# Decoding weights in place, squaring into another tile, a shorter layer norm, and a new table of event times

## The chip, the cores and the metric

The kernel runs on one core of a Trainium2 chip. The metric is the device time of one execution in microseconds (us), the median of several runs. Five engines work side by side: TensorE (PE, with its weight loads shown apart as PEld), VectorE (DVE), ScalarE (ACT), GpSimd (POOL) and SyncE (SP, whose queue issues all DMAs here). Each works through its own list of instructions in order and waits on semaphores for the others.

## The reference

A linear attention with decay over 4 batches, 8 heads, 768 steps and 48 channels gives 3072 tokens of 384 channels. Two feed-forward layers follow.

```python
def _attn_ref(r, k, v, w, u):
    ...
        cur = np.einsum('bhd,bhe->bhde', u[None] * kt, vt)
        y[:, :, t] = np.einsum('bhd,bhde->bhe', rt, state + cur)
        state = wt[:, :, :, None] * state + np.einsum('bhd,bhe->bhde', kt, vt)

def _moe_ref(x, w_in, w_out, g_ln):          # 384 -> 1024 -> 384
    h = x @ w_in
    e = np.exp(h - np.max(h, axis=-1, keepdims=True))
    solu = h * e / (np.sum(e, axis=-1, keepdims=True) + 1e-09)
    mu = np.mean(solu, axis=-1, keepdims=True)
    var = np.mean((solu - mu) ** 2, axis=-1, keepdims=True)
    return ((solu - mu) / np.sqrt(var + 1e-06) * g_ln) @ w_out

def _moe2_ref(x, w_in, w_out):               # 384 -> 2048 -> 384
    r = np.maximum(x @ w_in, 0.0)
    return (r * r) @ w_out
```

The weights arrive as 64-bit floats. The kernel reads each as two 32-bit words (`low`, `high`) and rebuilds a 32-bit float from their bits.

## The kernel before

Tokens go through in 24 tiles of 128 (`st`) and 12 groups of two tiles (`g`). Every float32 product is made of three matmuls on a high and a low part (`mm3`).

Per tile, attention runs as `prep_k` (two scans on DVE over the decays, behind the load of `wt`), `prep_r`, `prep_chk`, `prep_c*`, `u1` (transposes `pk`), `u3` (`pat`), `u2` (products `pm`, then the state's update on DVE), `u4` (outputs `py`, summed to `tk` or `early`) and `u5` (transposes `px`, split on ACT and DVE into `xh` and `xl`). The first layer is `m1_in` (18 matmuls `ph`, the logits, in PSUM banks of tag `h`), then maximum, exponential, product `z`, Square, variance, power -1/2 on POOL, `m1_ln` (normalises `z`) and `ln_T` (8 transposes `pl`, split into `lnh` and `lnl`). Per group, `m1_out` makes three products `po` of 24 matmuls, split into `x2h` and `x2l`; `m2_in(g, j)` makes 18 matmuls `p` and from them `gh` and `gl`; `m2_out(g, j)` adds 12 matmuls into `acc` (for group 0 `acch`, which takes the same banks of tag `h` as the logits); j runs from 0 to 7.

All weights stay in SBUF. They are loaded raw and decoded during the first tiles: `split_w1i`, `split_w1o` and `split_w2` call `decode` for pieces of 512 columns (384 for `w1o`), 38 pieces in all. A piece takes two or three ACT passes, two or three DVE passes and one POOL subtraction. It is rebuilt in a tile `t` of the tag `raw`, which has `RAWB` = 4 buffers and also holds `gh`, `gl` and the output tiles:

```python
        t = p2.tile([128, 512], F32, tag="raw", name="t", bufs=RAWB)[:, 0:n]
        nc.scalar.activation(out=t, in_=high.bitcast(F32), func=AF.Copy, scale=2.0 ** -112)
```

The order is written as a list of events: `at(t, f, *args)` enters a function with a time, the list is sorted by time, and the functions are called in that order. The tile framework's scheduler may still interleave the instructions of neighbouring events. Tables (`SPLIT_AT`, `ATT_AT`, `FIRST_AT`, `ATT_OFF`) set the times; `SHIFT` is read by `at` and empty.

Of the kernel before, what the change touches and what calls it, by code (L numbers as in the profile page):

```python
# [52 lines left out]
def body(ctx: ExitStack, tc: tile.TileContext, wrk, tok, vst, u, w1i, w1o, gln, w2, gen, vt, ug, out):  # L53
    nc = tc.nc
# [82 lines left out]
    def split_w1i(k):
        raw = raw_t.pop(("i", k))  # L140
        for a in range(0, FF1, 512):
            b = a + 512
            decode(raw[:, a:b], w1i_s[:, 0, k, a:b], w1i_s[:, 1, k, a:b])

    def split_w1o(k):
        raw = raw_t.pop(("o", k))
        for i in range(4):
            q = 4 * k + i
            decode(raw[:, i * DM:(i + 1) * DM], w1o_s[:, 0, q], w1o_s[:, 1, q], gcol[:, q:q + 1])

    def split_w2(j):
        if j < 7:
            raw = raw_t.pop(("2", j))
            parts = [raw[:, i:i + 512] for i in range(0, 1536, 512)]
        else:
            src = w2[j].rearrange("p (n t) -> p n t", t=2)
            parts = []
            for tag, a, n in (("lnh", 0, 1024), ("lnl", 1024, 512)):
# [2 lines left out]
                parts += [raw[:, i:i + 512] for i in range(0, n, 512)]
        w2_t[j] = wp.tile([128, 2, 1536], F32R, tag=f"w2_{j}", name="w2_s")
        for i, part in enumerate(parts):
            s = slice(i * 512, (i + 1) * 512)
            decode(part, w2_t[j][:, 0, s], w2_t[j][:, 1, s])

# [186 lines left out]
    def m1_in(st):  # L353
        xh, xl = x_t.pop(st)
        ph = ps_h.tile([128, FF1], F32, tag="h", name="ph")
        for n in range(2):
# [17 lines left out]
        z_t[st] = (z, nmz, rs, va, qq)  # L374

    def m1_ln(st):
        z, nmz, rs, va, qq = z_t[st]
        nc.vector.tensor_tensor(out=qq, in0=va, in1=rs, op=ALU.mult)
        nc.vector.tensor_scalar(out=z, in0=z, scalar1=nmz, scalar2=qq, op0=ALU.add, op1=ALU.mult)

    def ln_T(st):
# [2 lines left out]
        if g not in ln_t:
            ln_t[g] = (
                p1.tile([128, 8, 256], F32R, tag="lnh", name="lnh"),
                p1.tile([128, 8, 256], F32R, tag="lnl", name="lnl"),
            )
# [129 lines left out]
    wk = [(split_w1i, k) for k in range(3)] + [(split_w1o, k) for k in range(2)]
    wk += [(split_w2, j) for j in range(8)]
    refill = {0: 0, 1: 1, 2: 2, 6: 3, 5: 4, 8: 5, 7: 6}  # L520
    for n, (f, k) in enumerate(wk):
        at(SPLIT_AT[n], f, k)
# [147 lines left out]
```

## Time and profile before

| | us |
|---|---|
| three timed runs | 836.26, 837.32, 840.6 |
| median | 837.32 |
| the profiled execution, its own time | 832.33 |
| its span in the profile | 830.6 |

The profiled execution was 5.0 us below the median of the timed runs. 1.7 us of its time lie outside the span. In the profile an instruction is named by line, engine, operation and `out<-in`; a time in brackets is how long its engine stood idle just before it, and what ended that.

### The profile page before, as it was taken

What the parts mean: (1) busy time and instruction counts of PE and PEld (TensorE: products, weight loads), DVE (VectorE), ACT (ScalarE), POOL (GpSimd) and SP (SyncE); (2) the same over time, 40 slices, a digit from 0 to 9 for tenths busy, and PEclk for the clock granted to TensorE, in tenths of its full rate; (3) what the DMA queues carried; (4) which work ended last, traced back from release to release, by engine and by line L of the source; (5) the groups of instructions that cost most, each with busy time, mean ns of one, the idle gap of its engine ahead of it and who ended that gap; (6) DMA issues with size and microseconds to landing.
All of it is one profiled execution on the core that took longest, in us unless ns stands there. A gap on an engine that the chain in (4) does not pass through costs nothing.

```text
span 830.6 us, 17797 instructions
## 1 busy us (share of the span) xinstructions
PE 754.0 (91%) x7610; PEld 702.6 (85%) x7610; DVE 520.8 (63%) x974; ACT 338.2 (41%) x631; POOL 152.3 (18%) x146
## 2 busy tenths in 40 slices
PE   3566859899999999999999999999999999999996
PEld 3355759799788998988998999988998998999996
DVE  6899996775746556556556557556557557544332
ACT  4576566444423433333433333333333342333232
POOL 3635453231011011011011011011011011010000
PEclk9967978999999999999999999999999999999999
DMA  9940552221122202112112112112112112010000
GB/s 329 357 141 20 186 191 77 54 63 54 49 82 63 55 29 82 54 29 83 54 30 82 54 30 82 54 30 83 54 39 73 54 49 63 2 39 2 1 20 24
DMA packets 20568, 60.51 MB, mean 73 GB/s; under 512 B 3585, under 2 KB 12929, under 8 KB 18817
## 3 DMA queue, kind: packets, MB, share of 16 engines
q1 hardware_dynamic: 20480, 59.29, 22.5%
q8 instruction: 62, 1.02, 0.5%
q14 instruction: 26, 0.20, 0.1%
HBM read 54.56 MB, written 4.72 MB: 71 GB/s over the span
## 4 chain that ended last, share of the span: by engine, by line
PE 53%; DVE 22%; DMA 9%; ACT 6%; issue 3%; POOL 3%; SPq 2%; DVEq 0%; ACTq 0%; POOLq 0%
PE p L85 16%; PE acc L85 13%; DMA wt<-in_wrk 9%; PE po L85 7%; PE ph L85 7%; DVE q L232 3%; PE py L85 3%; PE pl L394 2%; DVE q L240 2%; SPq L207 2%; DVE p L433 2%; DVE t L114 2%; DVE t L112 1%; DVE stat L362 1%; PE acch L85 1%
## 5 line engine op out<-in xcount | busy, mean ns | idle before, releaser
L85 PE MATMUL p<-x2h,w_s 128*128 128x256 f32 x1152 | 222.8, 284 | 0.0
L85 PEld LDWEIGHTS p<-x2h,w_s 128*128 128x128 f32 x1152 | 184.3, 190 | 2.2
L85 PE MATMUL acc<-w_s,gh 128*128 128x384 f32 x704 | 185.3, 343 | 0.9 <-ACT gh L432 0.8
L85 PE MATMUL p<-x2l,w_s 128*128 128x256 f32 x576 | 162.2, 282 | 0.0
L85 PEld LDWEIGHTS acc<-w_s,gh 128*128 128x128 f32 x704 | 122.8, 189 | 2.9 <-ACT gh L432 1.3
L85 PE MATMUL acc<-w_s,gl 128*128 128x384 f32 x352 | 118.9, 339 | 1.0 <-DVE gl L434 1.0
L85 PE MATMUL po<-lnh,w1o_s 128*128 128x256 f32 x576 | 107.8, 282 | 7.9 <-DVE x2l L414 6.6
L85 PEld LDWEIGHTS p<-x2l,w_s 128*128 128x128 f32 x576 | 109.2, 190 | 1.0 <-DVE x2l L414 0.2
L431 ACT ACTIVATE r<-p 128x512 f32<-128x512 f32 x96 | 57.0, 594 | 126.0 <-PE p L85 95.5
L433 DVE TENSOR_TENSOR p<-p,r 128x512 f32<-128x512 f32 x96 | 66.7, 695 | 62.1 <-ACT r L431 62.0
L85 PE MATMUL ph<-w1i_s,xh 128*128 128x512 f32 x288 | 96.2, 415 | 6.5 <-ACT w1i_s L118 4.1
L85 PEld LDWEIGHTS po<-lnh,w1o_s 128*128 128x128 f32 x576 | 91.0, 190 | 10.6 <-DVE x2l L414 8.7
L259 POOL TENSOR_TENSOR tk<-tk 128x384 f32<-128x384 f32 x22 | 25.2, 1145 | 332.4 <-DMA tk<-in_tok 254.6
L85 PE MATMUL po<-lnl,w1o_s 128*128 128x256 f32 x288 | 80.8, 281 | 0.0
L434 DVE TENSOR_TENSOR gl<-p,gh 128x512 fp32r<-128x512 f32 x96 | 66.2, 690 | 10.8 <-ACT gh L432 4.5
L85 PEld LDWEIGHTS ph<-w1i_s,xh 128*128 128x128 f32 x288 | 56.0, 199 | 18.7 <-ACT w1i_s L118 4.6
L85 PEld LDWEIGHTS acc<-w_s,gl 128*128 128x128 f32 x352 | 66.2, 189 | 1.7 <-DVE gl L434 1.7
L85 PE MATMUL ph<-w1i_s,xl 128*128 128x512 f32 x144 | 59.9, 416 | 6.7 <-DVE xl L346 6.7
L432 ACT ACTIVATE gh<-r 128x512 fp32r<-128x512 f32 x96 | 61.0, 635 | 4.5 <-POOL w_s L119 2.3
L364 ACT ACTIVATE z<-ph,stat 128x1024 f32<-128x1024 f32 x24 | 26.8, 1116 | 77.3 <-DVE stat L362 77.3
L232 DVE TENSOR_TENSOR_SCAN q<-wt,d 112x520 f32<-112x520 f32 x22 | 28.3, 1284 | 46.6 <-DMA wt<-in_wrk 46.5
L85 PEld LDWEIGHTS po<-lnl,w1o_s 128*128 128x128 f32 x288 | 54.5, 189 | 0.0
(113 smaller groups left out, 1129.1 us busy)
## 6 DMA issues: line engine op xcount, KB each, us to landing
wt<-in_wrk SPq DMA_DIRECT2D x22, 675.9 KB, 4.8
raw<-in_w SPq DMA_DIRECT2D x7, 1536.0 KB, 8.6
tk<-in_tok SPq DMA_DIRECT2D x22, 384.0 KB, 3.2
vb<-in_tok SPq DMA_DIRECT2D x24, 192.0 KB, 2.4
vs<-in_vst SPq DMA_DIRECT2D x48, 96.0 KB, 2.7
out<-osb SPq DMA_DIRECT2D x24, 192.0 KB, 1.9
raw<-in_w1i SPq DMA_DIRECT2D x3, 1024.0 KB, 9.1
raw<-in_w1o SPq DMA_DIRECT2D x2, 1536.0 KB, 11.6
```

Source lines behind the costliest of these rows:

```text
L85: nc.tensor.matmul(o, l, r, start=start, stop=stop)
L114: nc.vector.scalar_tensor_tensor(out=ti, in0=high, scalar=-(1 << 31), in1=ti, op0=ALU.bitwise_and, op1=ALU.bitwise_or)
L207: nc.sync.dma_start(out=vs[64 * i:64 * i + 64], in_=vst[st, 64 - 64 * i:128 - 64 * i].rearrange("p (a c d) -> p a c d", a=NP, c=2))
L232: nc.vector.tensor_tensor_scan(out=q[:, WLEN - 1:0:-1], data0=wt[:, WLEN - 1:0:-1], data1=d1[:, WLEN - 1:0:-1], initial=0.0, op0=ALU.mult, ...
L240: nc.vector.tensor_tensor_scan(out=q[:, 0:WLEN - 1], data0=wt[:, 0:WLEN - 1], data1=d1[:, 0:WLEN - 1], initial=0.0, op0=ALU.mult, op1=ALU.add)
L259: nc.gpsimd.tensor_tensor(out=rk, in0=rk, in1=tk[:, 1], op=ALU.mult)
L364: nc.scalar.activation(out=z, in_=ph, func=AF.Exp, bias=nm, accum_out=se)
L394: nc.tensor.transpose(pl[:, f, :], z[:, f0:f0 + 128], ident)
L431: nc.scalar.activation(out=r, in_=p, func=AF.Relu)
L432: nc.scalar.activation(out=gh, in_=r, func=AF.Square)
L433: nc.vector.tensor_tensor(out=p, in0=p, in1=r, op=ALU.mult)
L434: nc.vector.tensor_tensor(out=gl, in0=p, in1=gh.bitcast(F32), op=ALU.subtract)
```

## The change

- **Decode by pieces, in place.** `decode` now works in the raw tile itself: ACT scales `high` in place and `low` in place, DVE joins them in two passes, and the last one writes into `high` (every second word of the tile). Every piece takes the same two ACT and two DVE passes. `parts` then copies the high part (ACT) and subtracts (POOL), reading every second word. `dec` and `par` are events of their own for each piece. `w1o` goes in 4 pieces of 768 columns in place of 8 of 384, so there are 34 pieces. `w2[7]` is fetched by an event of its own.
- **Squares elsewhere.** The Square of the layer norm writes its elements to `lnh` in SBUF, the tile that `ln_T` fills later, and no more to the logits' banks `ph`.
- **Layer norm without the softmax's sum.** The factor 1/sum is taken out of the fraction: the variance gets 1e-6 times the squared sum added, and the reciprocal and two products with it go. Six one-column DVE instructions per tile become four.
- **Order.** `SHIFT` gets some 170 entries for single events, `STEADY` some 30 that hold for every later tile or group, and one time in `SPLIT_AT` moves.

```diff
-SPLIT_AT = (-21, -18, -15, -14, -11.5, -5.5, -2.5, -1.5, -1, 1, 3, 7.5, 10)
+SPLIT_AT = (-21, -18, -15.5, -14, -11.5, -5.5, -2.5, -1.5, -1, 1, 3, 7.5, 10)
-SHIFT = {}
+SQUARE_ACT = 0
+DEC_STEP = 0.2
+SHIFT = {
+    ('dec', '2', 0, 0): 0.03, ('dec', '2', 0, 1): -0.31, ('dec', '2', 1, 2): -0.8, ('dec', '2', 2, 0): 0.69,
...
+STEADY = {
...
+    ('m2_in', 0): 0.43, ('m2_in', 2): 0.33, ('m2_in', 7): 0.19, ('m2_out', 2): -0.02, ('m2_out', 3): -0.43,
...
-    n_dec = [0]
-
-    def decode(raw, hi, lo, scale=None):
-        n = raw.shape[1]
+    def decode(raw):
         low, high = raw[:, :, 0], raw[:, :, 1]
-        t = p2.tile([128, 512], F32, tag="raw", name="t", bufs=RAWB)[:, 0:n]
-        ti = t.bitcast(I32)
-        nc.scalar.activation(out=t, in_=high.bitcast(F32), func=AF.Copy, scale=2.0 ** -112)
-        n_dec[0] += 1
-        if n_dec[0] % 4 == 0:
-            nc.vector.tensor_scalar(out=ti, in0=ti, scalar1=3, scalar2=None, op0=ALU.logical_shift_left)
-            nc.vector.scalar_tensor_tensor(
-                out=ti, in0=low, scalar=29, in1=ti, op0=ALU.logical_shift_right, op1=ALU.bitwise_or)
-        else:
-            nc.scalar.activation(out=low, in_=low.bitcast(U32), func=AF.Copy, scale=0.93 * 2.0 ** -29)
-            nc.vector.scalar_tensor_tensor(
-                out=ti, in0=ti, scalar=3, in1=low, op0=ALU.logical_shift_left, op1=ALU.bitwise_or)
+        nc.scalar.activation(out=high.bitcast(F32), in_=high.bitcast(F32), func=AF.Copy, scale=2.0 ** -112)
+        nc.scalar.activation(out=low, in_=low.bitcast(U32), func=AF.Copy, scale=0.93 * 2.0 ** -29)
         nc.vector.scalar_tensor_tensor(
-            out=ti, in0=high, scalar=-(1 << 31), in1=ti, op0=ALU.bitwise_and, op1=ALU.bitwise_or)
-        if scale is not None:
-            nc.scalar.activation(out=t, in_=t, func=AF.Copy, scale=scale)
+            out=low, in0=high, scalar=3, in1=low, op0=ALU.logical_shift_left, op1=ALU.bitwise_or)
+        nc.vector.scalar_tensor_tensor(
+            out=high, in0=high, scalar=-(1 << 31), in1=low, op0=ALU.bitwise_and, op1=ALU.bitwise_or)
+
+    def parts(raw, hi, lo, gains=()):
+        t = raw[:, :, 1].bitcast(F32)
+        for s, g in gains:
+            nc.scalar.activation(out=t[:, s], in_=t[:, s], func=AF.Copy, scale=g)
         nc.scalar.copy(out=hi, in_=t)
         nc.gpsimd.tensor_tensor(out=lo, in0=t, in1=hi.bitcast(F32), op=ALU.subtract)
...
-        nc.vector.tensor_scalar(out=rs, in0=se, scalar1=1e-9, scalar2=None, op0=ALU.add)
-        nc.vector.reciprocal(out=rs, in_=rs)
         nc.vector.tensor_scalar(out=nmz, in0=sz, scalar1=-1.0 / FF1, scalar2=None, op0=ALU.mult)
-        nc.scalar.activation(out=ph, in_=z, func=AF.Square, bias=nmz, accum_out=ss)
-        nc.vector.tensor_scalar(out=va, in0=ss, scalar1=1.0 / FF1, scalar2=rs, op0=ALU.mult, op1=ALU.mult)
-        nc.vector.tensor_scalar(out=va, in0=va, scalar1=rs, scalar2=1e-6, op0=ALU.mult, op1=ALU.add)
+        nc.vector.tensor_scalar(out=se, in0=se, scalar1=1e-9, scalar2=None, op0=ALU.add)
+        nc.vector.tensor_scalar(out=e2, in0=se, scalar1=1e-6, scalar2=se, op0=ALU.mult, op1=ALU.mult)
+        nc.scalar.activation(
+            out=ln_t[g][0][:, :, t * 128:(t + 1) * 128], in_=z.rearrange("p (f n) -> p f n", f=8),
+            func=AF.Square, bias=nmz, accum_out=ss)
+        nc.vector.tensor_scalar(out=va, in0=ss, scalar1=1.0 / FF1, scalar2=e2, op0=ALU.mult, op1=ALU.add)
         nc.gpsimd.tensor_tensor(out=va, in0=va, in1=mhalf, op=ALU.pow)
...
-        nc.vector.tensor_tensor(out=qq, in0=va, in1=rs, op=ALU.mult)
-        nc.vector.tensor_scalar(out=z, in0=z, scalar1=nmz, scalar2=qq, op0=ALU.add, op1=ALU.mult)
+        nc.vector.tensor_scalar(out=z, in0=z, scalar1=nmz, scalar2=va, op0=ALU.add, op1=ALU.mult)
...
     def at(t, f, *args):
-        ev.append((t + SHIFT.get((f.__name__, *args), 0), len(ev), f, args))
+        name = f.__name__
+        t += SHIFT.get((name, *args), 0)
+        if args[0] not in ("i", "o", "2") and args[0] >= (3 if len(args) == 2 else 6):
+            t += STEADY.get((name, args[0] % 2 if len(args) == 1 else args[1]), 0)
+        ev.append((t, len(ev), f, args))
```

On PE, the first place is where the logits of tile 3 are done and the outputs `acch` of group 0 begin, ahead of the first `po` of group 1. Before:

```order
L85 MATMUL p<-x2h,w_s 128x256
L85 MATMUL acch<-w_s,gh 128x384 x2
L85 MATMUL acch<-w_s,gl 128x384
L85 MATMUL acch<-w_s,gh 128x384 x2
L85 MATMUL acch<-w_s,gl 128x384
L85 MATMUL acch<-w_s,gh 128x384
L394 MATMUL pl<-ident,z 128x128 x8
```

Of the change, the end of a run of 25 matmuls `acch` that follows the last `p` there, and what comes behind it:

```order
L129 MATMUL acch<-w_s,gh 128x384 x2
L129 MATMUL acch<-w_s,gl 128x384
L129 MATMUL acch<-w_s,gh 128x384
L430 MATMUL pl<-ident,z 128x128 x8
L129 MATMUL acch<-w_s,gh 128x384
L129 MATMUL acch<-w_s,gl 128x384
```

Ahead of the first `po` of group 1 there stood 50 matmuls `p` and 13 `acch`; now there stand 70 and 34. On DVE, of weights worth 36 pieces of 512 columns, 26 were decoded ahead of that group's first `x2l` before, and 30 are now.

On DVE, the second place is tile 1's attention: the maximum of tile 0's logits (`stat<-ph`), the scans of tile 2 (`q<-early,d_89`), and the state's updates, on which the outputs `py` of tile 1 wait. Before:

```order
L362 TENSOR_REDUCE stat<-ph 128x1
L232 SCALAR_TENSOR_TENSOR q<-early,d_89 112x520
L236 RECIPROCAL d_89<-q 112x8
L237 COPY pc<-q 112x8
L239 TENSOR_TENSOR early<-early,q 112x512
L316 TENSOR_TENSOR state<-q,pm 112x192
L240 SCALAR_TENSOR_TENSOR q<-early,d_89 112x520
L314 TENSOR_TENSOR q<-state,pc 112x4x48
L365 SCALAR_TENSOR_TENSOR z,stat<-ph,z 128x1024
L316 TENSOR_TENSOR state<-q,pm 112x192
```

Of the change:

```order
L268 SCALAR_TENSOR_TENSOR q<-early,d_89 112x520
L401 TENSOR_REDUCE stat<-ph 128x1
L352 TENSOR_TENSOR state<-q,pm 112x192
L272 RECIPROCAL d_89<-q 112x8
L350 TENSOR_TENSOR q<-state,pc 112x4x48
L273 COPY pc<-q 112x8
L275 TENSOR_TENSOR early<-early,q 112x512
L352 TENSOR_TENSOR state<-q,pm 112x192
L276 SCALAR_TENSOR_TENSOR q<-early,d_89 112x520
```

Both state updates and the product between them now stand ahead of the second scan. The two additions to `early<-py` for tile 2 also stand together now, ahead of the product `z` of tile 1; before, `z` stood between them.

On PE, the third place is an even tile of the steady part (tile 10): `px`, and the `po` of the group before. Before, two of the three `po` of the group stood ahead of `px` and the third behind four matmuls `acc`:

```order
L85 MATMUL po<-lnh,w1o_s 128x256
L342 MATMUL px<-ident,tk 128x128 x3
L85 MATMUL acc_3302<-w_s,gh 128x384 x2
L85 MATMUL acc_3302<-w_s,gl 128x384
L85 MATMUL acc_3303<-w_s,gh 128x384
L85 MATMUL po<-lnh,w1o_s 128x256
L85 MATMUL po<-lnl,w1o_s 128x256
```

Of the change, two `po` follow `px` at once, then 18 matmuls `p`, the third `po` and the logits:

```order
L129 MATMUL acc_3225<-w_s,gl 128x384
L129 MATMUL acc_3226<-w_s,gh 128x384 x2
L129 MATMUL acc_3226<-w_s,gl 128x384
L378 MATMUL px<-ident,tk 128x128 x3
L129 MATMUL po<-lnh,w1o_s 128x256
L129 MATMUL po<-lnl,w1o_s 128x256
```

All `po` of a group now stand behind `px`, with a whole `p` between the second and the third. In the odd tiles `px`, 12 matmuls `acc` and `ph` follow one another as before, and so do the scan, `wt<-wt,q`, `p<-p,r` and `xl<-px,xh` on DVE.

## Rows read from the trace of the kernel before

**Rows 1.** The page: busy time, and 40 slices of PE and its granted clock.
```profile
PE 754.0 (91%) x7610; PEld 702.6 (85%) x7610; DVE 520.8 (63%) x974; ACT 338.2 (41%) x631; POOL 152.3 (18%) x146
...
PE   3566859899999999999999999999999999999996
...
PEclk9967978999999999999999999999999999999999
```

**Rows 2.** Windows by stage: PE, PEld, DVE, ACT, POOL busy, clock, DMA share, GB/s.
```profile
24.60:97.00 72.40, 50.61 (x497) 40.10 (x497) 65.18 (x115) 48.82 (x94) 35.34 (x30) 0.83 0.50 163
97.00:127.50 30.50, 21.11 (x156) 19.02 (x155) 26.89 (x46) 18.11 (x34) 16.00 (x11) 0.75 0.48 178
127.50:200.00 72.50, 67.96 (x672) 64.83 (x672) 50.56 (x83) 34.79 (x63) 23.21 (x17) 0.96 0.23 69
200.00:830.60 630.60, 606.83 (x6158) 572.21 (x6156) 361.27 (x702) 227.32 (x426) 67.83 (x72) 1.00 0.16 48
```

**Rows 3.** Timeline of DVE, 42 to 56 us: start, duration, instruction.
```profile
47.66 0.34 DVE L316 TENSOR_TENSOR state<-q,pm 112x192 f32<-112x192 f32 x1
...
49.61 0.33 DVE L314 TENSOR_TENSOR q<-state,pc 112x192 f32<-112x192 f32 x1
```

**Rows 4.** Timeline of PE, 97 to 128 us, with idle time and its end.
```profile
112.04 0.28 PE L85 MATMUL p<-x2h,w_s 128*128 128x256 f32 x1
119.47 1.01 PE L85 MATMUL acch<-w_s,gh 128*128 128x384 f32 x2 [7.16 <-ACT ph L370]
...
123.84 1.97 PE L394 MATMUL pl<-ident,z 128*128 128x128 f32 x8 [1.76 <-DVE z L379]
...
127.53 0.41 PE L85 MATMUL po<-lnh,w1o_s 128*128 128x256 f32 x1
```

**Rows 5.** Timeline of all engines, 112 to 124 us.
```profile
113.54 1.20 DVE L365 SCALAR_TENSOR_TENSOR z<-ph,z 128x1024 f32<-128x1024 f32 x1
...
118.19 1.09 ACT L370 ACTIVATE ph<-z,stat 128x1024 f32<-128x1024 f32 x1
...
121.50 1.27 POOL L119 TENSOR_TENSOR w_s<-t,w_s 128x512 fp32r<-128x512 f32 x1
...
121.57 1.22 DVE L378 TENSOR_TENSOR stat<-stat 128x1 f32<-128x1 f32 x1 [0.72 <-POOL stat L373]
```

**Rows 6.** Windows with a low granted clock, columns as in the stages above.
```profile
116.00:128.60 12.60, 7.37 (x27) 6.87 (x28) 9.21 (x19) 7.83 (x15) 3.64 (x4) 0.50 0.35 125
166.00:170.00 4.00, 4.00 (x18) 4.00 (x18) 3.97 (x6) 2.44 (x6) 2.25 (x2) 0.59 0.34 100
```

**Rows 7.** Groups by line and shape: count, busy us, mean ns, idle before.
```profile
L114 DVE SCALAR_TENSOR_TENSOR t<-raw,t 128x512 int32<-128x512 int32 x27 | 22.9, 862 | 0.2
L103 ACT ACTIVATE t<-raw 128x512 f32<-128x512 f32 x27 | 17.8, 670 | 16.3 <-POOL w_s L119 8.6 <-PE acc L85 3.1 <-POOL w1o_s L119 2.5
...
L239 DVE TENSOR_TENSOR wt<-wt,q 112x512 f32<-112x512 f32 x22 | 15.1, 687 | 0.0
...
L111 ACT ACTIVATE raw<-raw 128x512 int32<-128x512 uint32 x21 | 14.1, 676 | 0.0
...
L106 DVE TENSOR_SCALAR t<-t 128x512 int32<-128x512 int32 x7 | 4.1, 586 | 0.5 <-ACT t L103 0.5
...
L114 DVE SCALAR_TENSOR_TENSOR t<-raw64s,t 128x512 int32<-128x512 int32 x3 | 2.0, 680 | 0.0
```

**Rows 8.** Who PE waited for, 200 us to the end: total, times, longest.
```profile
PE ph L85 <- DVE xl L346: 6.7, 8, 1.2
PE po L85 <- DVE x2l L414: 6.6, 5, 1.9
PE pl L394 <- DVE z L379: 1.6, 5, 0.4
```

**Rows 9.** The chain that ended last, 268 to 282 us: start, us, work.
```profile
271.89 2.06 PE p L85 x18
273.95 2.08 PE acc L85 x12
```

More of the change, by code (lines that the diff above doesn't have):

```diff
@@ L43 @@
 RAWB = 4
-SHIFT = {}
+SQUARE_ACT = 0
+DEC_STEP = 0.2
+SHIFT = {
[7 rows of a table added]
+    ('ln_T', 2): 0.24, ('ln_T', 3): 0.22, ('ln_T', 4): 0.25, ('load_tok', 6): 0.94, ('load_vb', 1): -0.07,
+    ('load_vb', 3): -0.31, ('load_vb', 4): 1.15, ('load_vb', 5): 1.26, ('load_vb', 6): 0.31, ('load_vb', 7): -0.33,
+    ('load_vs', 2): 0.29, ('load_vs', 4): 1.15, ('load_vs', 6): 0.31, ('load_vs', 7): -0.42, ('load_vs', 8): -0.43,
[14 rows of a table added]
+    ('prep_c', 2): 0.58, ('prep_c', 4): 1.15, ('prep_c', 6): 0.31, ('prep_c', 7): -0.42, ('prep_c', 9): -0.28,
+    ('prep_c2', 4): 1.15, ('prep_c2', 6): 0.31, ('prep_c2', 7): -0.42, ('prep_c3', 4): 1.15, ('prep_c3', 6): 0.31,
+    ('prep_c3', 7): -0.42, ('prep_chk', 4): 1.43, ('prep_chk', 5): 0.4, ('prep_chk', 6): 0.02,
+    ('prep_chk', 7): -0.42, ('prep_k', 0): -3.41, ('prep_k', 2): 0.08, ('prep_k', 4): 1.15, ('prep_k', 6): 0.31,
+    ('prep_k', 7): -0.42, ('prep_r', 4): 1.15, ('prep_r', 6): 0.31, ('prep_r', 7): -0.42, ('u1', 1): -1,
[4 rows of a table added]
+}
+STEADY = {
+    ('load_vb', 0): 0.91, ('load_vb', 1): -0.56, ('load_wrk', 0): -0.64, ('load_wrk', 1): -0.64, ('m1_ln', 0): 0.01,
[5 rows of a table added]
+}
 SLOT0 = 6
@@ L137, in fetch_w2 @@
             fetch(("2", j), (5, 6, 7, 6, 5, 6, 7)[j], w2[j], nc.sync)
[L139 to L154, printed above, removed]
         else:
             src = w2[j].rearrange("p (n t) -> p n t", t=2)
-            parts = []
             for tag, a, n in (("lnh", 0, 1024), ("lnl", 1024, 512)):
@@ L160, in split_w2, with piece, dec, par @@
                 nc.sync.dma_start(out=raw, in_=src[:, a:a + n])
[L161 to L165, printed above, removed]
+                raw_t["2", j, a] = raw
+    def piece(kind, k, i):
+        if kind == "i":
+            s = slice(512 * i, 512 * i + 512)
+            return raw_t[kind, k][:, s], w1i_s[:, 0, k, s], w1i_s[:, 1, k, s]
+        if kind == "o":
+            q = 4 * k + 2 * i
+            gains = [(slice(n * DM, (n + 1) * DM), gcol[:, q + n:q + n + 1]) for n in range(2)]
+            hi, lo = (w1o_s[:, n, q:q + 2].rearrange("p a n -> p (a n)") for n in range(2))
+            return raw_t[kind, k][:, 2 * i * DM:2 * (i + 1) * DM], hi, lo, gains
+        if k not in w2_t:
+            w2_t[k] = wp.tile([128, 2, 1536], F32R, tag=f"w2_{k}", name="w2_s")
+        s = slice(512 * i, 512 * i + 512)
+        raw = raw_t[kind, k][:, s] if k < 7 else raw_t[kind, k, 0][:, s] if i < 2 else raw_t[kind, k, 1024]
+        return raw, w2_t[k][:, 0, s], w2_t[k][:, 1, s]
+    def dec(*key):
+        decode(piece(*key)[0])
+    def par(*key):
+        parts(*piece(*key))
     wt_t, tk_t, q_t, kt_t, y_t, x_t, c_t = {}, {}, {}, {}, {}, {}, {}
@@ L359, in m1_in @@
                 mm3(ph[:, s], xh[:, k], xl[:, k], w1i_s[:, 0, k, s], w1i_s[:, 1, k, s], k == 0, k == 2)
-        stat = sm.tile([128, 8], F32, tag="stat", name="stat", bufs=2)
-        nm, se, sz, rs, nmz, ss, va, qq = (stat[:, i:i + 1] for i in range(8))
+        stat = sm.tile([128, 7], F32, tag="stat", name="stat", bufs=2)
+        nm, se, sz, e2, nmz, ss, va = (stat[:, i:i + 1] for i in range(7))
+        g, t = st // 2, st % 2
+        if g not in ln_t:
+            ln_t[g] = [p1.tile([128, 8, 256], F32R, tag=tag, name=tag) for tag in ("lnh", "lnl")]
         nc.vector.tensor_reduce(out=nm, in_=ph, axis=AX.X, op=ALU.max, negate=True)
@@ L366, in m1_in @@
             out=z, in0=ph, scalar=1.0, in1=z, op0=ALU.mult, op1=ALU.mult, accum_out=sz)
-        nc.vector.tensor_scalar(out=rs, in0=se, scalar1=1e-9, scalar2=None, op0=ALU.add)
-        nc.vector.reciprocal(out=rs, in_=rs)
         nc.vector.tensor_scalar(out=nmz, in0=sz, scalar1=-1.0 / FF1, scalar2=None, op0=ALU.mult)
-        nc.scalar.activation(out=ph, in_=z, func=AF.Square, bias=nmz, accum_out=ss)
-        nc.vector.tensor_scalar(out=va, in0=ss, scalar1=1.0 / FF1, scalar2=rs, op0=ALU.mult, op1=ALU.mult)
-        nc.vector.tensor_scalar(out=va, in0=va, scalar1=rs, scalar2=1e-6, op0=ALU.mult, op1=ALU.add)
+        nc.vector.tensor_scalar(out=se, in0=se, scalar1=1e-9, scalar2=None, op0=ALU.add)
[4 more added lines that the diff above has]
+        nc.vector.tensor_scalar(out=va, in0=ss, scalar1=1.0 / FF1, scalar2=e2, op0=ALU.mult, op1=ALU.add)
         nc.gpsimd.tensor_tensor(out=va, in0=va, in1=mhalf, op=ALU.pow)
-        z_t[st] = (z, nmz, rs, va, qq)
+        z_t[st] = (z, nmz, va)
     def m1_ln(st):
-        z, nmz, rs, va, qq = z_t[st]
-        nc.vector.tensor_tensor(out=qq, in0=va, in1=rs, op=ALU.mult)
-        nc.vector.tensor_scalar(out=z, in0=z, scalar1=nmz, scalar2=qq, op0=ALU.add, op1=ALU.mult)
+        z, nmz, va = z_t[st]
+        nc.vector.tensor_scalar(out=z, in0=z, scalar1=nmz, scalar2=va, op0=ALU.add, op1=ALU.mult)
     def ln_T(st):
@@ L383, in ln_T @@
         g, t = st // 2, st % 2
[L384 to L388, printed above, removed]
         lh, ll = ln_t[g]
@@ L432, in m2_in @@
         nc.scalar.activation(out=gh, in_=r, func=AF.Square)
-        nc.vector.tensor_tensor(out=p, in0=p, in1=r, op=ALU.mult)
+        if g < SQUARE_ACT:
+            nc.scalar.activation(out=p, in_=r, func=AF.Square)
+        else:
+            nc.vector.tensor_tensor(out=p, in0=p, in1=r, op=ALU.mult)
         nc.vector.tensor_tensor(out=gl, in0=p, in1=gh.bitcast(F32), op=ALU.subtract)
@@ L517, in body @@
         at(tj + 1.7, m2_end, g)
[L518 to L522, printed above, removed]
+    wk = [("i", k, 2) for k in range(3)] + [("o", k, 2) for k in range(2)] + [("2", j, 3) for j in range(8)]
+    refill = {0: 0, 1: 1, 2: 2, 6: 3, 5: 4, 8: 5, 7: 6, 11: 7}
+    for n, (kind, k, pieces) in enumerate(wk):
+        for i in range(pieces):
+            at(SPLIT_AT[n] + DEC_STEP * i, dec, kind, k, i)
+            at(SPLIT_AT[n] + DEC_STEP * (i + 1) + 0.01, par, kind, k, i)
         if n in refill:
```

28 rows, old and new, of tables (SHIFT, STEADY) are left out of this document.

## The prediction, on record before the changed kernel ran

> **What bounds the kernel now.** I read the page first: PE is busy for 754 of 830.6 us, and the slices with gaps and with a low granted clock all lie in the first quarter [rows 1]. Then windows by stage. From 200 us on PE idles 23.8 of 630.6 us [rows 2], 13.3 of it in two kinds of wait [rows 8]; from 24.6 to 97 it idles 21.8, from 97 to 127.5 it idles 9.4, from 127.5 to 200 it idles 4.5 [rows 2]. In the two stages up to 127.5 DVE is busy for 65.2 of 72.4 and 26.9 of 30.5 us: there DVE, which decodes the weights beside attention and layer norm, sets the pace and PE waits. From 127.5 on PE sets it. So a gain can only come from PE's gaps, 59.5 us from 24.6 us on, and from matmuls that run at a half clock; all work that the change takes from DVE, ACT or POOL behind 200 us is free either way.
>
> **The change, part by part.**
>
> *Decoding.* DVE loses the third pass of every fourth piece: 7 of 586 ns for 512 columns, 4.1 us [rows 7], two shorter ones, and the fixed share of four pieces fewer. ACT gets `low` scaled for those nine pieces too, 9 x 0.68 = 6 us at most [rows 7], while it idles 36 of 103 us from 24.6 to 127.5 [rows 2]; 0, as that slack hides it (without it, 6). ACT stood idle 16.3 us ahead of the 27 rows `t<-raw`, for POOL or PE to give back a buffer of the tag `raw` [rows 7]. Decoding in place ends that wait and those of `gh` and `gl` for `t`. No row shows a DVE write to every second word. The nearest: ACT writing every second word takes 676 ns against 670 to contiguous ones, and DVE reading every second word takes 680 against 687 for an instruction on contiguous words [rows 7]. I take 0; the far bound is as much again as the columns cost, some 0.55 us for each of 68 instructions.
>
> *Work put into the hole.* The longest wait of PE is 7.16 us ahead of `acch`, for the Square in the logits' banks, and 1.76 us follow for `z` ahead of `pl` [rows 4]. The product `z`, the other reader of the banks, starts at 113.54 and ends at 114.75; the Square starts at 118.19 [rows 5], because ACT's queue holds casts and `gh` that wait on POOL ahead of it. With the Square in `lnh` the banks come free 4.5 us earlier. The order uses that: 20 more `p` and 21 more `acch` stand ahead of `po`, 20 x 0.114 + 21 x 0.173 = 5.9 us [rows 9]. The hole of 8.9 us can take them if DVE keeps its pace; by the same count of instructions DVE has decoded four pieces more at that point, which is what it saved. **Term A: -5.9** (0 if `z` comes later by as much, -8.9 at most).
>
> *Square's new wait.* It now needs `lnh` free of the group before. In the steady order all `po` stand ahead of the next `ph`, so it is free. For tile 2 the Square stands behind `po` of group 0; right behind it in ACT's queue stands the cast of the last `po`, which waits for the same matmuls, so little is held up. 0, and some 3 us at most, an estimate: the Square of 1.09 us [rows 5] with what follows it up to `z` comes behind the last `po` in place of beside it.
>
> *State ahead of the scan.* `py` of tile 1 waits for the state's two updates. In the trace the product for the second stands behind a scan and starts at 49.61, the first update at 47.66 [rows 3]. The new order puts both ahead of that scan: `px` of tile 1 comes some 2 us earlier, and that of tile 2 about as much, as its additions go ahead of `z`. DVE sets the pace there, so part of it comes back as a wait for something else. **Term B: -2** (0 to -4).
>
> *Layer norm.* Two one-column instructions fewer between Square and `pl`, some 0.3 us per tile; from 200 us on PE waits 1.6 us in 5 places for `z` [rows 8], of which it takes most: **term F: -1** (0 to -1.6). One of those removed, the product with 1/sum, took 1.22 us for one column in tile 3, from just after POOL began a subtraction until that ended, 121.50 + 1.27 [rows 5]. Taken as its own cost, the removal would give 1.2 us more ahead of `pl`. The Trainium skill (SBUF — State Buffer, "Who interferes with whom") says that DVE's second pair of ports is shared with GpSimd under an exclusive lock, and that the loser waits for the whole instruction; the row agrees, and by that rule `z`, next on DVE, would be held in its place, and the sum would be without those 1.2 us. I count 0, the end at which POOL's work stays where it is.
>
> *Clock.* From 116 to 128.6 us, behind the long wait, PE ran at a granted 0.50, its lower level of 1.2 GHz, and was busy for 7.37 us [rows 6]; at the full clock those take half. With the hole filled the clock may stay up. **Term C: -2** (0 to -3.7).
>
> *After the first po of group 1.* Six pieces are left to decode in place of ten, so the 4.5 us of PE idle from 127.5 to 200 [rows 2] and the low clock from 166 to 170 [rows 6] (1.6 us at most) should shrink in that ratio. **Term D: -2.4** (0 to -6.1).
>
> *Steady order.* PE waits 6.6 us in 5 places for `x2l` ahead of `po`, and 6.7 in 8 for `xl` ahead of `ph` [rows 8]. The first kind is the third `po`, four `acc` behind the second, which needs a PSUM buffer that DVE still reads. Now a `p` of 2.06 us [rows 9] stands between, so it goes: **term E: -6.6** (0 to -6.6). The second kind sits in the odd tiles, where neither PE's nor DVE's order changes: 0 (-6.7 at most). On SP the stores of a group now go ahead of one load of values, which is double-buffered: 0.
>
> Sum: 5.9 + 2 + 1 + 2 + 2.4 + 6.6 = 19.9 us. From the profiled execution's 832.3 that makes 812.4. The median of the timed runs is 1.006 times the profiled time, so **817 us** as a median, 2.4% faster.
>
> **Rivals.** All times as medians.
> 1. *The front stays DVE's.* POOL's and ACT's share moves, but DVE is as full as before, `z` of tile 3 comes late by what PE has done ahead, and A, C and D come to nothing. For it: DVE at 90% and 88% in those stages. Against: the wait of 7.16 us is one for ACT, not for DVE. B, E and F are left: 9.6 us, 828.
> 2. *The steady part gives nothing.* `x2l` of the first `po` now stands behind a scan that waits for its load, and the third `po` finds the wait again. For it: the same scan makes `xl` late in odd tiles. Against: 4.8 us of PE work (`po` and `p`) more lie between. Without E: 13.3 us, 824.
> 3. *It doesn't do what it says.* The scheduler's order is right for its own estimates, and what is gained at the hole is lost at new ones; the place most likely is the Square's wait in tile 2 and the first scaling of `w2[7]`, which waits in ACT's queue for a load ahead of `gh`. 0 to 4 us: 835.
> 4. *Slower: writes to every second word.* If DVE's in-place writes cost 0.55 us more each, the 60 ahead of the first `x2l` of group 1 add 33 us to an engine with 10.8 us idle from 24.6 to 127.5 [rows 2]. 22 us later, A to D gone, E and F kept: +14.6, 852. It decides from about 0.3 us per instruction, where 60 x 0.3 - 10.8 eats E and F. For it: no row shows the write. Against: ACT's writes and DVE's reads of that kind cost nothing. The Trainium skill (SBUF — State Buffer, "Door 1: The DMA port swizzle") puts a float32 stride of up to four words as free, but no run here shows it for a DVE write; by it this rival would not come about.
>
> **How the numbers follow.** The forecast, 811 to 823, gets 0.46; rivals 1 and 2 get 0.17 each, as each needs one part of the mechanism to fail; rival 3 gets 0.10; rival 4 gets 0.07, since the rows beside it speak against; a time below 811, with `ph`'s waits gone too or the 21.8 us before 97 half closed, gets 0.03. Runs of this kernel differ by up to 0.5%, and about that much is what a measurement can tell from none. Faster by over 0.5% (below 833.1) are the forecast, rivals 1 and 2 and the better case: 0.83; rival 3 is the same: 0.10; rival 4 is slower: 0.07. The range 806 to 833 leaves out rival 4, half of rival 3 and some of the better case, under 0.2.
>
> **What would show it.** The wait ahead of `acch` for the Square is gone, and PE has 5 to 6 us more behind it at the first `po` of group 1 (A); PE's granted clock stays at 1.00 from some 112 us on (C); no wait of `po` for `x2l` from 200 us on while those of `ph` for `xl` in odd tiles stay at about 1 us each (E); `py` of tile 1 follows `pm` some 2 us sooner (B); decode passes on DVE take 0.68 us where POOL is idle (rival 4 wrong). The prediction is wrong if those passes take 0.9 us or more, if `z` of tile 3 comes no earlier than now while PE waits 5 us for it, or if PE still idles 20 us or more from 200 us to the end of the span.

## The result and the profile after

| | before | changed |
|---|---|---|
| timed runs, us | 836.26, 837.32, 837.73, 840.6 | 807.59, 808.07, 808.09, 810.66 |
| median | 837.53 | 808.08 |
| the profiled execution | 832.33 | 807.59 |

The ratio is 0.965 (95% interval 0.962 to 0.968): 3.5% faster. 817 was forecast, with a range of 806 to 833. By the profiled executions, against which the sum was made, 24.7 us went where the sum said 19.9. The profiled execution of before was a quick one of its kind, 5 us under its median; that of the changed kernel is 0.5 us under its median. So the two medians lie 4.7 us further apart than the two traces; in which part of the kernel the quick execution was quick isn't shown. The changed kernel was timed once, in four runs, and the median of before moved by up to 1.4 us from set to set (837.5 to 838.9), so differences to the changed kernel from other sets carry about as much.

The page of the changed kernel, as in [rows 1]:

```profile
PE 745.6 (93%) x7610; PEld 700.3 (87%) x7610; DVE 517.1 (64%) x909; ACT 341.2 (42%) x628; POOL 158.0 (20%) x142
...
PE   3377888999999999999999999999999999999996
...
PEclk9858889999999999999999999999999999999999
```

Windows of the changed kernel, columns as in [rows 2, 6]:

```profile
97.00:105.00 8.00, 8.00 (x84) 7.26 (x84) 7.02 (x10) 4.01 (x7) 5.84 (x4) 0.50 0.32 105
116.00:128.60 12.60, 8.77 (x50) 8.25 (x49) 10.81 (x20) 8.24 (x16) 9.05 (x6) 0.90 0.35 125
126.00:128.60 2.60, 2.60 (x11) 2.60 (x12) 2.44 (x5) 1.29 (x3) 0.00 (x0) 0.51 0.03 14
132.00:200.00 68.00, 66.73 (x699) 62.70 (x699) 46.39 (x83) 31.07 (x57) 20.32 (x17) 1.00 0.28 83
200.00:805.80 605.80, 591.01 (x6078) 563.40 (x6076) 360.03 (x650) 222.51 (x418) 72.20 (x71) 1.00 0.17 49
```

The half clock is not gone, most of it has moved: from 116 to 128.6 us [rows 6] to 97 to 105. From 200 us to the end PE idles 14.8 us, before 23.8 [rows 2]. Who PE waited for in that part of the changed kernel, as in [rows 8]:

```profile
PE ph L129 <- DVE xl L382: 6.6, 7, 1.3
PE pm L129 <- DVE z L404: 0.8, 1, 0.8
PE pl L430 <- DVE z L420: 0.3, 1, 0.3
PE pk L316 <- DVE lnl L433: 0.2, 1, 0.2
```

The wait of `po` for `x2l` is gone, that of `ph` for `xl` stays as it was.

**Where the time came from.** Two traces with other orders can't be laid side by side by time. I compare them by equal work: every matmul weighs as much as the usual distance to the next of its kind (`p` and `po` 0.114 us, `acc` and `acch` 0.173, `ph` and the transposes 0.22 to 0.23, the small ones of attention 0.03 to 0.06), and the lead is how much sooner the changed kernel has done what the kernel before had done at a given time. It carries a few tenths of error.

| at (us of before) | 60 | 110 | 120 | 130 | 150 | 170 | 200 | 270 | 450 | 630 | 810 |
|---|---|---|---|---|---|---|---|---|---|---|---|
| lead, us | -2.7 | -1.3 | 4.4 | 7.7 | 2.8 | 7.1 | 9.4 | 15.1 | 19.1 | 24.0 | 25.0 |

Nothing is won up to 110 us, 9.4 by 200 (the terms A to D: 12.3), and 15.6 behind it (E and F: 7.6).

### The profile page after: what moved, and what is told of

The parts are those of the page before. It is cut to its first block, busy times and chain, and to the rows that moved or that the text cites. A ratio compares the mean times of both kernels' runs of the same rounds, so it can differ in the third digit from the quotient of the medians.

```text
span 805.8 us, 17754 instructions
## 1 busy us (share of the span) xinstructions
PE 745.6 (93%) x7610; PEld 700.3 (87%) x7610; DVE 517.1 (64%) x909; ACT 341.2 (42%) x628; POOL 158.0 (20%) x142
## 4 chain that ended last, share of the span: by engine, by line
PE 72%; DMA 10%; DVE 10%; ACT 3%; POOL 2%; SPq 1%; issue 1%; ACTq 0%; DVEq 0%; POOLq 0%
PE p L129 22%; PE acc L129 19%; PE po L129 11%; PE ph L129 10%; DMA wt<-in_wrk 5%; PE py L129 3%; PE pl L430 3%; DMA raw<-in_w1i 2%; PE pat L129 2%; DVE q L268 2%; POOL w_s L155 1%; DVE raw L145 1%; DMA raw<-in_w 1%; PE acch L129 1%; SPq L243 1%
## 5 line engine op out<-in xcount | busy, mean ns | idle before, releaser
L129 PE MATMUL acc<-w_s,gh 128*128 128x384 f32 x704 | 182.9, 341 | 0.0
L129 PE MATMUL po<-lnh,w1o_s 128*128 128x256 f32 x576 | 104.0, 279 | 1.3 <-DVE lnl L433 1.2
L129 PEld LDWEIGHTS po<-lnh,w1o_s 128*128 128x128 f32 x576 | 88.9, 188 | 2.2 <-DVE lnl L433 1.7
L415 POOL TENSOR_TENSOR stat<-stat,mhalf 128x1 f32<-128x1 f32 x24 | 14.3, 597 | 196.6 <-DVE stat L414 196.6
```

The lines of the kernel that those rows point to most:

```text
L129: nc.tensor.matmul(o, l, r, start=start, stop=stop)
```

## Experiments

Theory 1 is that PE's order brings the gain by leaving no wait, and that the code edits only allow that order; theory 2, that the code edits bring it themselves. All times are medians beside runs of the kernel before on the same chip (837.7, 838.8 and 838.9 in the three sets). "Lead" is as above.

**The two tables, and the code without them.**

```diff
-SHIFT = { ... }
-STEADY = { ... }
+SHIFT = {}      # e1, e3
+STEADY = {}     # e1, e2
```

> The changed kernel with both tables of event times empty: in-place decoding by pieces, the Square in lnh and the shorter layer norm stay. Theory 1 (the gain is an order on PE that leaves no wait, and the code edits only allow it): po waits for x2l again in the later groups, and the hole at tile 3 is shorter by the Square's 4.5 us but not filled; with some 3 us from the waits ahead of pl that makes 837.5 - 4.5 - 3 = 830 us. Theory 2 (the code edits bring the gain, the tables little): 808 to 812 us. That nothing of the code matters: 837 us.

Measured: 828.06 us, ratio 0.989 (0.986 to 0.993). The lead is 3.7 us at 200 and 4.6 at the end; `po` again waits 6.7 us in 5 places for `x2l`. Theory 1 comes nearer (830 us against 808 to 812), but 9.6 of the 29.4 us are there without any table, so the code edits bring some of the gain themselves.

> The changed kernel with the table for the later tiles and groups (STEADY) empty; one entry of the other table is set to that of its neighbours (u2 of tile 7, -0.42), so that the order of events stays a legal one. By the prediction's term E, which counted the idle time shown ahead of po, the time rises by 6.6 us, to 815. Theory 1 says that each such wait costs PE more than its idle time, since the matmuls around it start late as well: some 13 of the 16 us that the changed kernel gains behind 200 us are lost, 821 us. Theory 2: 808 to 810 us.

Measured: 822.01 us, 13.9 above the changed kernel. Behind 200 us, this kernel's waits on PE:

```profile
PE ph L122 <- DVE xl L375: 5.8, 7, 1.2
PE po L122 <- DVE x2l L443: 4.8, 5, 1.4
PE po L122 <- DVE at L324: 2.1, 1, 2.1
```

> The changed kernel with the table for single events (SHIFT) empty and STEADY kept. Theory 1: the front's lead of some 9.5 us at 200 us goes but for the Square's part of up to 4.5: 813 to 818 us, and no wait of po for x2l behind 200 us. Theory 2: 808 to 810 us.

Measured: 813.93 us, 5.9 above the changed kernel; the lead is 4.8 at 200 and 18.4 at the end, and no `po` waits for `x2l`. So STEADY is worth about twice the idle time that it takes away, and SHIFT 5.9.

**STEADY alone**, in the kernel before:

```diff
+STEADY = { ... }
...
+        if not name.startswith("split") and args[0] >= (3 if len(args) == 2 else 6):
+            t += STEADY.get((name, args[0] % 2 if len(args) == 1 else args[1]), 0)
```

> The kernel before with nothing but the STEADY table added, from tile 6 and group 3 on. Two orders of matmuls alone, no code edit. By term E of the prediction (the idle time shown ahead of po) 6.6 us go: 837.5 - 6.6 = 831 us. Theory 1 (a wait costs more than its idle time, the table is worth what the changed kernel loses without it, 822.0 - 808.1 = 13.9 us): 824 us. If the table only works together with the shorter layer norm: 834 us or more.

Measured: 824.83 us, ratio 0.984 (0.979 to 0.990), 14.0 less. The table needs none of the code edits. Against the quick trace of before, only 9.8 of it show behind 200 us (the lead goes from -1.6 to 8.2): the waits of `po` are gone, those of `ph` for `xl` have grown from 6.7 to 10.3 us.

Why twice? I compare seven groups of equal work, from `px` of tile 9 to that of tile 23. Before, and then the changed kernel (window; span, PE, PEld, DVE and so on):

```profile
325.00:755.00 430.00, 418.46 (x4372) 394.86 (x4371) 258.54 (x501) 157.72 (x297) 54.29 (x56) 1.00 0.17 51
```

```profile
309.85:730.07 420.22, 413.65 (x4373) 393.68 (x4372) 262.91 (x473) 158.06 (x297) 59.21 (x56) 1.00 0.18 52
```

9.8 us went. Idle time fell by 5.0 (11.54 to 6.57), and as many matmuls were busy for 4.8 us less. The other kernels without the table take 429.5 to 433.0 us for this work (e1, e2, e6, e12), all with it 420.9 to 424.0. Busy time holds part of a wait: around one, matmuls start further apart than usual. Here, in the kernel before, `po` started 1.25 us behind the last `acc`, where 0.17 is usual, and only 0.92 of it is shown as idle:

```profile
421.05 0.34 PE L85 MATMUL acc<-w_s,gh 128*128 128x384 f32 x1
422.30 0.39 PE L85 MATMUL po<-lnh,w1o_s 128*128 128x256 f32 x1 [0.92 <-DVE x2l L414]
```

In the seven groups the steps from `acc` to `po` took 5.4 us more than usual, where 4.6 are shown as idle, those from `acc` to `pl` 2.5, where 1.4 are shown, and `po` behind `po` 1.6 more than in the changed kernel (118 ns apart against 115). The second part is not the table's: in e2, without the table but with the shorter layer norm, those steps are as usual. The table's own worth is therefore read from e2, which takes 9.3 us more than the changed kernel for the seven groups: 5.7 in the steps from `acc` to `po` (4.9 shown as idle), 1.6 in `po` behind `po`, and most of the rest in `p` and `acc` a little further apart. So a wait for `x2l` cost some 1.2 times what is shown. For the rest of the table's worth the traces show where it lies and no cause.

**The Square's place.** Back to the banks, and alone in the kernel before:

```diff
-            out=ln_t[g][0][:, :, t * 128:(t + 1) * 128], in_=z.rearrange("p (f n) -> p f n", f=8),
+            out=ph, in_=z,                                   # e4; e6 is the reverse, in the kernel before
             func=AF.Square, bias=nmz, accum_out=ss)
```

> The changed kernel with only the Square written to the logits' banks again. The prediction's term A rests on the Square's place: by it acch waits again, and 4.5 to 5.9 us come back, 812.5 to 814 us. Theory 1 (the order fills the hole, the Square's place matters little): the Square of tile 3 ran from 118.40 to 119.56 us while acch began at 118.39, so acch would start 1.2 us later, and the wait of 3.06 us for z ahead of pl behind it takes that up: 808 to 809.3 us.

Measured: 812.37 us, 4.3 more than the changed kernel. Theory 1 missed here and term A's mechanism was right: the scheduler sets other instructions round the moved one, and PE waits for the Square again, at 73.98 and 124.27 us:

```profile
PE acch L129 <- ACT ph L411: 5.4, 1, 5.4
...
PE ph L129 <- ACT ph L411: 3.5, 1, 3.5
```

By the lead against the changed kernel, 2.3 us are lost at 200 us and some 5 at 240, so more than these two waits is in it: PE waits 1.18 us for `gh` at 211.97, and from 215 to 220 us it ran at a granted 0.77.

> The kernel before with only the Square's elements written to lnh in place of the logits' banks. Term A's mechanism: the banks come free 4.5 us earlier, and PE's wait of 7.16 us ahead of acch shrinks by that: 833 us. Rival (the place is worth nothing by itself, since the wait of 1.76 us for z behind it grows by as much): 837 us. The code edits all together gave 9.6 us, 828.

Measured: 839.08 us, ratio 1.002 (0.999 to 1.004): nothing. The wait is still there, 4.45 us in place of 7.16, but has another releaser. DVE of this kernel, then PE:

```profile
117.35 2.03 DVE L240 TENSOR_TENSOR_SCAN q<-wt,d 112x520 f32<-112x520 f32 x1
119.30 1.19 DVE L365 SCALAR_TENSOR_TENSOR z<-ph,z 128x1024 f32<-128x1024 f32 x1
```

```profile
120.65 0.98 PE L85 MATMUL acch<-w_s,gh 128*128 128x384 f32 x2 [4.45 <-DVE stat L367]
```

The product `z`, the other reader of the banks, now stands behind a scan and ends at 120.5; before it ended at 114.75 [rows 5]. That is rival 1's mechanism, in a kernel with one part of the change.

**Decoding in place alone**, in the kernel before:

```diff
-        t = p2.tile([128, 512], F32, tag="raw", name="t", bufs=RAWB)[:, 0:n]
+        t = high.bitcast(F32)
...
+            out=low, in0=high, scalar=3, in1=low, op0=ALU.logical_shift_left, op1=ALU.bitwise_or)
...
+            out=high, in0=high, scalar=-(1 << 31), in1=low, op0=ALU.bitwise_and, op1=ALU.bitwise_or)
```

> The kernel before with only its decode done in place, in two ACT and two DVE passes for every piece, at the times and in the pieces of before. Rival 4 (writes to every second word are dear) gave 852 us; the changed kernel's passes of 0.68 us speak against. All code edits together gave 9.6 us and the Square alone nothing; if the rest is the decoding (a pass fewer in every fourth piece, 4.1 us of DVE, and no waits for a buffer of the tag raw): 829 to 833 us. If the front keeps DVE's pace all the same: 836 to 838 us.

Measured: 836.32 us, ratio 0.997 (0.994 to 0.999): 2.6 us, next to nothing. Its trace has waits of 5.6 us ahead of `acch` and 4.1 ahead of `ph`, both for the Square in the banks. Writes to every second word cost nothing here: from 105 to 111 us, with POOL at rest, the changed kernel's passes take as long as contiguous ones did [rows 7].

```profile
105.00:111.00 6.00, 6.00 (x32) 4.89 (x32) 4.77 (x8) 5.67 (x11) 0.00 (x0) 0.95 0.92 343
```

```profile
108.15 0.68 DVE L145 SCALAR_TENSOR_TENSOR raw<-raw 128x512 int32<-128x512 int32 x1
...
109.82 1.29 DVE L147 SCALAR_TENSOR_TENSOR raw<-raw 128x512 int32<-128x512 int32 x2
```

**The layer norm of before**, in the changed kernel:

```diff
+        nc.vector.tensor_scalar(out=rs, in0=se, scalar1=1e-9, scalar2=None, op0=ALU.add)
+        nc.vector.reciprocal(out=rs, in_=rs)
...
+        nc.vector.tensor_scalar(out=va, in0=ss, scalar1=1.0 / FF1, scalar2=rs, op0=ALU.mult, op1=ALU.mult)
+        nc.vector.tensor_scalar(out=va, in0=va, scalar1=rs, scalar2=1e-6, op0=ALU.mult, op1=ALU.add)
...
+        nc.vector.tensor_tensor(out=qq, in0=va, in1=rs, op=ALU.mult)
```

> The changed kernel with the layer norm of before (reciprocal of the sum, six one-column instructions), the Square still in lnh. The prediction's term F gives back 1 us at most 1.6: 809 us, and its term for the removed product is 0. From the run e8 the odd tiles' chain from xl to pl has next to no slack in the changed kernel; by that two instructions of some 0.15 us cost 0.3 us in each of 9 odd tiles behind 200 us: 811 us. If the shorter layer norm is worth nothing: 808 us.

Measured: 821.59 us, 13.5 more than the changed kernel, and no theory had it. Against the changed kernel the lead is 0.0 us at 60, -10.4 at 100, -9.9 at 200 and -13.0 at 750. Tile 1 shows how. The old layer norm, DVE and then POOL:

```profile
77.09 0.20 DVE L413 TENSOR_SCALAR stat<-stat 128x1 f32<-128x1 f32 x1
77.21 1.93 DVE L276 TENSOR_TENSOR_SCAN q<-wt,d 112x520 f32<-112x520 f32 x1
79.06 0.18 DVE L414 TENSOR_SCALAR stat<-stat 128x1 f32<-128x1 f32 x1
...
81.23 0.16 DVE L420 TENSOR_TENSOR stat<-stat 128x1 f32<-128x1 f32 x1 [0.45 <-POOL stat L415]
81.31 0.55 DVE L301 TENSOR_REDUCE c<-tk 128x8 f32<-128x384 f32 x1
81.77 0.80 DVE L421 TENSOR_SCALAR z<-z,stat 128x1024 f32<-128x1024 f32 x1
```

```profile
78.00 2.23 POOL L155 TENSOR_TENSOR w_s<-raw,w_s 128x512 fp32r<-128x512 f32 x1
80.20 1.00 POOL L415 TENSOR_TENSOR stat<-stat,mhalf 128x1 f32<-128x1 f32 x1
```

The changed kernel at the same place, DVE:

```profile
74.03 0.16 DVE L414 TENSOR_SCALAR stat<-stat 128x1 f32<-128x1 f32 x1
...
75.95 1.47 DVE L420 TENSOR_SCALAR z<-z,stat 128x1024 f32<-128x1024 f32 x1 [0.45 <-POOL stat L415]
```

From the first one-column instruction behind the Square to the normalising of `z` it takes 4.7 us (77.09 to 81.77) against 1.9 (74.03 to 75.95). Not the 0.2 us of each instruction counts here, but what stands ahead of it in its queue: the second waits behind a scan of 1.9 us, so POOL's power gets behind a subtraction of 2.2 us, and the third lets a reduction in ahead of `z`. PE's wait for this `z` grew from 1.32 to 3.27 us. That is one step of several: the lead was already -3.1 at 74 us, and goes from -7.3 at 84 to -10.4 at 100 us. How much each takes, and how much of it is the scheduler's other order, isn't separated.

**Mending the changed kernel.** Four orders meant to beat it.

```diff
-LOADS = (... 'Y0', 'O0', 'T1', 'I2', 'G', ...)
+LOADS = (... 'Y0', 'I2', 'T1', 'O0', 'G', ...)            # e7
+    ('m1_in', 1): 0.35,                                   # e8, e9, e10, in STEADY
-    ('m1_ln', 1): 0.01,
+    ('m1_ln', 1): 0.4, ('ln_T', 1): 0.4,                  # e9, e10, in STEADY
+    # e10, in SHIFT: dec and par of ('2', 4, 0) and ('2', 4, 2) 0.8, of ('2', 4, 1) 1.6 in place of 0.81
```

> The changed kernel with the third load of w_in issued ahead of the first of w_out (I2 and O0 change places in LOADS), so that its decoding stands ahead of that of w_out on ACT and DVE. Term B failed at this place: PE's first logits wait 8.8 us for the cast of w1i_s, which stands behind four passes of 1.7, 1.3, 1.7 and 1.0 us for w_out on DVE. If that wait is on the path, some 4 to 5 us of it go: 803 to 804 us. If the front is DVE's (the same passes come later all the same): 808 us.

Measured: 821.72 us, 13.6 worse. The wait for the cast of `w1i_s` fell from 8.8 to 2.4 us, and `pm` of tile 1 ended at 40. But on DVE the state's update went behind four passes over `w_out`, the whole layer norm of tile 0 and a scan, and PE waited for it:

```profile
50.09 2.32 DVE L420 TENSOR_SCALAR z<-z,stat 128x1024 f32<-128x1024 f32 x1 [0.45 <-POOL stat L415]
52.34 0.34 DVE L352 TENSOR_TENSOR state<-q,pm 112x192 f32<-112x192 f32 x1
```

```profile
52.73 0.44 PE L129 MATMUL py<-q,rt 48*64 48x48 f32 x2 [12.75 <-DVE state L352]
```

> The changed kernel with one entry more in STEADY: the logits of odd tiles 0.35 later, so that the 18 p of 2.07 us stand ahead of ph in place of behind it. The 7 waits of ph for xl (0.66 to 1.31 us each, 6.6 in all) then end under p. If the logits' lateness finds nothing behind it: 808.1 - 6.6 - 7 x 0.17 = 800 us. If z is now late ahead of pl, whose slack behind ph shrinks by 2.07 us: part of it comes back, 803 to 808 us.

Measured: 814.29 us, 6.2 worse. All waits for `xl` are gone, and behind 200 us one has come for them:

```profile
PE pl L430 <- DVE z L420: 9.7, 10, 1.5
```

> The changed kernel with the logits of odd tiles 0.35 later, as in the run before, and z's normalising and the transposes pl of odd tiles 0.4 later too, so that between ph and pl again 18 p, 12 acc and 18 p stand. If the run before lost because pl came closer behind ph (9.7 us of waits for z in 10 places): no waits for xl and none for z, 808.1 - 6.6 - some 1 = 800 us. If the chain from xl to z is late for another reason, and po now waits for lnl: 806 us or more.

Measured: 809.76 us, ratio to before 0.966 (0.963 to 0.969): the same as the changed kernel. The waits for `xl` are gone and `z` is late by 0.7 us in 2 places only, but `pk` now follows `pl` closely and waits for `lnl`, 3.6 us in 9 places, and PE is busy longer for the equal work of above:

```profile
310.46:731.56 421.10, 417.64 (x4372) 396.67 (x4371) 262.22 (x473) 157.29 (x297) 57.57 (x56) 1.00 0.18 52
```

The idle time is 3.1 us shorter than in the changed kernel (6.57 to 3.46) and the busy time 4.0 us longer (413.65 to 417.64). The steps between the `ph` are 8.4 us shorter; nearly half of what came back is `pk` in the middle of `py`: the steps from `py` to `pk` take 4.1 us more than usual. `pk` behind the next `p` wasn't tried.

> The run e9 and one edit more in SHIFT: the three pieces of w2[4] decoded 0.8 later, which puts one subtraction fewer ahead of the power of tile 3 on POOL. In the changed kernel that power started 3.2 us late behind three subtractions of 5.76 us together, and PE waited 3.06 us for z ahead of pl. If that wait is on the path: 1.9 us less than e9, 798 us. If the front is paced by DVE and POOL whatever the order: the same as e9, within 0.5%.

Measured: 811.72 us, 2.0 more than e9, which is within the 0.5% that the expectation took for no difference. The wait ahead of `pl` did shrink, from 3.06 to 0.54 us. But the lead against the changed kernel is 0 at 130 us and -4.1 at 150: at 141.66 and 144.47 us PE waits 1.39 and 2.07 us for `x2h` and `x2l` (which stands behind a decode pass on DVE), and from 145 to 150 us it ran at a granted 0.66.

## Why the prediction was right, and where not, step by step

**Term A (-5.9): the mechanism was right, the size too large.** No wait for the Square is left ahead of `acch`, and the longer row of `p` and `acch` runs on. PE in the changed kernel:

```profile
118.39 0.51 PE L129 MATMUL acch<-w_s,gh 128*128 128x384 f32 x2
...
125.95 1.91 PE L430 MATMUL pl<-ident,z 128*128 128x128 f32 x8 [3.06 <-DVE z L420]
...
130.07 0.28 PE L129 MATMUL po<-lnh,w1o_s 128*128 128x256 f32 x1
```

The prediction's sum counted 20 more `p`, but the trace of before has 54 of them ahead of the first `po` of group 1 and not 50, so 16 more `p` and 21 more `acch` make 5.5 us. That `po` comes 2.5 us later than before [rows 4] with this work done: some 3 us won, A to C together; the lead is 3.4 us at 140. The wait ahead of `pl` grew from 1.76 to 3.06 us: `z` is normalised at 125.08 in place of 122.98, as its power stands behind three subtractions on POOL that take 5.76 us:

```profile
118.78 5.76 POOL L155 TENSOR_TENSOR w_s<-raw,w_s 128x512 fp32r<-128x512 f32 x3
124.50 0.55 POOL L415 TENSOR_TENSOR stat<-stat,mhalf 128x1 f32<-128x1 f32 x1
```

Undoing the Square's place costs 4.3 us (e4), making it alone gives nothing (e6), as `z` came late there: it counts only while `z` comes early.

**Term B (-2): wrong, 0 or a loss.** The wait of `py` of tile 1 for the state did shrink, from 7.5 us (5.98 and 1.49) to 2.83. What failed is the step that this would show at `px`: on DVE, four passes over `w_out` now stand ahead of the last two pieces of `w_in`, and the logits of tile 0 wait 9.4 us for these (8.83 and 0.59) where it was 4.8 (4.05 and 0.75); `px` of tile 1 starts at 54.58 us, before at 53.81; that of tile 2 comes 0.66 us earlier (68.82 against 69.48).

```profile
31.54 1.67 DVE L145 SCALAR_TENSOR_TENSOR raw<-raw 128x768 int32<-128x768 int32 x1
...
36.60 0.96 DVE L147 SCALAR_TENSOR_TENSOR raw<-raw 128x768 int32<-128x768 int32 x1
37.47 1.29 DVE L145 SCALAR_TENSOR_TENSOR raw<-raw 128x512 int32<-128x512 int32 x2
```

```profile
40.13 0.79 PE L129 MATMUL ph<-w1i_s,xh 128*128 128x512 f32 x1 [8.83 <-ACT w1i_s L154]
```

**Term C (-2): wrong, 0.** At the old hole PE ran at the full clock up to 126 us and then, behind the wait for `z`, at 0.51 to 128.6, so the sign that the clock stays at 1.00 from 112 us on failed too. It ran at 0.50 from 97 to 105 us, where it was busy for 8.00 us (7.37 in the old stretch). Ahead of that stretch it had waited 2.41 us, up to 95.72, for the state, whose update stood on DVE behind five decode passes (90.35 to 95.32). The step that failed is that one filled hole would keep the clock up: another wait of PE came ahead of another stretch at half clock, and the mean clock over the span is 0.97 in both.

**Term D (-2.4): right, too small.** From 132 to 200 us PE idles 1.3 us (4.5 before from 127.5 on), and the clock is 1.00 all the way. The lead rises from 3.4 at 140 to 9.4 at 200 us, 6.0, at the far bound of 6.1.

**Term E (-6.6): the mechanism was right, the price half.** The waits are gone; the table that removes them is worth 13.9 us (e2) or 14.0 (e5). The step that failed is to price the new order by the idle time shown ahead of `po` alone. In the seven groups the steps to `po` cost 5.7 us where 4.9 are shown, and 3.6 more lie in other matmuls that start further apart, of which the traces show no cause.

**Term F (-1) and the removed product (0).** F is the largest miss: 13.5 us by undoing it in e11, some 10 of them between 60 and 100 us; it wasn't run alone. "Some 0.3 us per tile" priced two instructions by their own time and counted them from 200 us on only, while in the front each stands in line on a full engine. That the product's own 1.22 us are not to be had is borne out at tile 1, not at tile 3: `z`, next in the queue, takes 1.47 us at 75.95, just behind the start of a product on POOL (75.88, 0.99 us long), in place of the 0.81 that it takes at 125.08 with POOL at rest. The Trainium skill (SBUF — State Buffer, "Who interferes with whom") says that whoever issues first holds the shared pair for its whole instruction. The trace agrees in kind: POOL came first, and `z` took 0.66 us longer, where POOL's product ran for another 0.92 us.

**Decoding (0) and the Square's new wait (0): about right.** Decoding in place alone gave 2.6 us (e12). The Square of tile 2 came at 93.73 us, before at 86.34, behind a scaling that had waited 2.62 us for a load of weights; but PE had other work, and `pl` of tile 2 follows at 99.34 without idle time.

**ph for xl: right** (6.6 us in 7 places), and e8 and e9 show that these waits are not to be had by moving `ph`.

**From the sum to the median.** The factor 1.006 between median and profiled time was one execution's luck; for the changed kernel it is 1.0006. It put 4.6 us on the sum where 0.5 were due: 4.1 of the 8.9 us between 817 and 808.1. The other 4.8 are E and F with D, too small by more than A, B and C were too large. So the total is nearer than its terms, by misses that offset one another.

**The rivals.** 1 (the front stays DVE's) is half true: it is what e6 shows, and what happened to B and, by the state's update, to C; in e12 PE waits for ACT's Square instead. 2 is refuted by the waits behind 200 us, 3 by the result, 4 by the passes of 0.68 us. The undone parts add up to 13.9 + 13.5 + 4.3 + 5.9 = 37.6 us, more than the 29.4 won, and three parts done alone to 14.0 + 2.6 + 0 = 16.6. The shorter layer norm and SHIFT weren't done alone, and the decoding wasn't undone. STEADY needs none of the others; of the front it is shown that the Square's place needs them.

What stays open: why `po` follow one another 118 ns apart in one order and 115 in another, and other matmuls with them; why e5 gains 14.0 us by its medians and 9.8 behind 200 us by its trace; and how much of the front's gain belongs to the layer norm itself and how much to the order that the scheduler builds round it.
